# Attention and MoE on one Trainium2 core: the scaled words of the weights' decoding go to a PSUM bank

## The chip, the cores and the metric

The kernel runs on one core of a Trainium2 chip. The metric is the device time of one execution in microseconds (us). Engines: TensorE (PE, with its weight loads PEld), VectorE (DVE), ScalarE (ACT), GpSimd (POOL) and SyncE (SP), which issues most DMA transfers.

## The reference

```python
# attention: q, k, v are (8 batches, 8 heads, 576, 64) in fp32
scores = scale * np.matmul(q, k.transpose(0, 1, 3, 2))
...
mask = (rel >= 0) & (rel < window)          # window = 128
scores = np.where(mask, scores + bias[None], -1000000000.0)
scores = scores - np.max(scores, axis=-1, keepdims=True)
attn = np.exp(scores)
attn = attn / (np.sum(attn, axis=-1, keepdims=True) + 1e-09)
return np.matmul(attn, v).astype(np.float32)
...
# MoE: x is the attention's output, (4608 tokens, 512)
h = x @ w_in                                # (512, 2048)
g = h * (1.0 / (1.0 + np.exp(-1.702 * h)))
return (g @ w_out).astype(np.float32)       # (2048, 512)
```

`bias` is a slope of each head times minus the distance of the two positions. `w_in` and `w_out` come in 64-bit floats.

## The kernel before, in words

**The work.** The FFN runs over chunks of 256 tokens. One *step* is one chunk with one of the 16 blocks of 128 hidden columns: twelve up products into an h_ps bank (L552), ScalarE's tanh (L557), VectorE's g (L558), a split of g in a high and a low part (gh on ScalarE L561, gl on GpSimd L562), and six down products into the two accumulators acc0 and acc1 (L571). All products run in fp32 by such splits, three products for one. A `Job` is a chunk with a range of blocks; the list of jobs sets the order of the steps: chunk 0 with blocks 0–7 (steps 0–7), chunk 1 with all 16 (8–23), chunk 0 with blocks 8–15 (24–31), chunk 2 from step 32, chunk 3 from step 48, and so on.

**The attention** is cut into units of a pair of heads, which feed the chunks' x. In the first two batches a "whole" unit takes 256, 256 or 64 queries: units 0–3 have queries 0–255 of batch 0 ("early"), 4–7 queries 256–511, 8–11 queries 512–575, and 12–23 are the same of batch 1. A unit passes stages: loads of q, k and V (`load`, `load_whole_v`), score products into s_ps and sb_ps (L324), bias and minimum on VectorE (L351), exponentials on ScalarE (L374), reciprocal and scaling (L392 to L402, shared out over three engines), transposes into t_ps (L419) with copies out to pw (L427), the mix, which is the product of pw with V (L476), and the copy of its result to x (L485). `tick` moves four units by a stage each; the main loop calls it by a pace worked out from when the chunks are due. The mix of units 4 and later goes to the tile x_ps, tag x_ps, one buffer; the early ones use the tag h_ps. From batch 2 on, `mix` and `sum_up` (L499, L520) use x_ps too.

**The weights.** `fetch_weights` (L199) loads a block of w_in and one of w_out, 512 KB each, as 64-bit words through SP's queue, in program order with the loads of the attention (`move`, L155). `decode` (L203) makes fp32 parts out of them, a *half* (one block of one matrix) at a time; w4 below stands for the two halves of block 4. ScalarE scales the top words with Prelu, so that the sign is kept and the exponent lands in its place (L211, into the tile wc, tag o, three buffers); VectorE shifts the low words by 29 (L212) and joins the two by a shift of wc by 3 and an or, in place (L213, "shift-and-or" below); ScalarE casts the result to the high part (L216); GpSimd subtracts that to the low part (L217). There are 32 halves. The first three are decoded inside the attention's first ticks (`DECODE_TICKS`), the rest in the main loop, spread by `need`; the first eight keep their place in the program (`pin`).

**The order.** A scheduler sets the order of each engine's instructions from the program, the tiles' dependencies and its own model of time; an engine runs its order strictly from the front. SP's loads keep program order. PSUM has eight banks, all in use: acc0, acc1, s_ps, two of t_ps, one of x_ps, two of h_ps. V of the whole units has three buffers (L264), and so have q and k (tags rq, rk).

Of the kernel before, what the change touches and what calls it, by code (L numbers as in the profile page):

```python
# [8 lines left out]
F32 = mybir.dt.float32  # L9
F32R = mybir.dt.float32r  # L10
BF16 = mybir.dt.bfloat16
I32 = mybir.dt.int32
I64 = mybir.dt.int64
AF = mybir.ActivationFunctionType
ALU = mybir.AluOpType
# [5 lines left out]
P = 128  # L21
# [121 lines left out]
def tile_kernel(ctx: ExitStack, tc: tile.TileContext, q0, k0, v0, qT, kT, v, w_in, w_out, out):  # L143
    nc = tc.nc
# [5 lines left out]
    ffn = ctx.enter_context(tc.tile_pool(name="ffn", bufs=2))  # L150
    ps = ctx.enter_context(tc.tile_pool(name="ps", bufs=1, space=PSUM))
# [51 lines left out]
    def decode(st, name, pin=lambda ins: ins):  # L203

        words = st.bitcast(I32).rearrange("p (m two) -> p m two", two=2)
        top, low = words[..., 1], words[..., 0]
        c = ffn.tile([P, 512], I32, name="wc", tag="o", bufs=3)

        pin(nc.scalar.activation(c.bitcast(F32), top.bitcast(F32), AF.Prelu, scale=2.0 ** -112, alpha=2.0 ** 32))  # L211
        pin(nc.vector.tensor_scalar(low, low, 29, None, ALU.logical_shift_right))  # L212
        pin(nc.vector.scalar_tensor_tensor(c, c, 3, low, ALU.logical_shift_left, ALU.bitwise_or))  # L213
        w = c.bitcast(F32)
        res = const.tile([P, 2, 512], F32R, name=name, tag=name)
        pin(nc.scalar.copy(res[:, 0], w))  # L216
        pin(nc.gpsimd.tensor_tensor(res[:, 1], w, res[:, 0].bitcast(F32), ALU.subtract))  # L217
        return res
# [425 lines left out]
    def decode_next():  # L644
        nonlocal halves
        g, ws = halves // 2, (w1, w2)[halves % 2]

        pin = [tc.keep_in_program_order] if halves < PINNED else []
        ws[g] = decode(ws[g], f"w{1 + halves % 2}_{g}", *pin)
        halves += 1  # L650
# [123 lines left out]
```

## Time and profile before

| | |
|---|---|
| median of 3 runs | 1064.5 us (1063.76 to 1065.91) |
| the profiled execution | 1068.36 us |
| its span | 1066.3 us |
| granted TensorE clock, mean | 0.995 |
| HBM read, written | 67.63 MB, 9.44 MB |
| DMA, mean over the span | 74 GB/s |
| first tanh of step 0, 8, 16, 32, 48 | 32.4, 93.3, 126.4, 192.9, 253.2 us |
| decoding, first and last Prelu | 19.3, 125.8 us |

How to read the profile: L is a line of the kernel. A group's row names line, engine, operation, "output tile <- input tiles" without buffer numbers, shape, and the count behind an x; then its busy time in us, the mean in ns, and the idle time of the engine just ahead with what ended it. In rows grouped by tile the three numbers are the shortest, median and longest duration in ns. Rows of the timeline begin with the start and the duration in us; several instructions of one line in a row are drawn together. In the views of waits "A <- B: 3.7, 5, 1.8" is A's wait for B in us, how often, and the longest; indented rows by tile name what an engine sat idle for ahead of that tile's instructions.

### The profile page before, as it was taken

Reading aid. Unit: us, or ns where it says so; the run is one execution under the profiler, and the core shown is the slowest. Engines: PE = TensorE matmul, PEld = TensorE weight load, DVE = VectorE, ACT = ScalarE, POOL = GpSimd, SP = SyncE. Lnnn points to the kernel's source line nnn. Section 1 sums busy time; section 2 is a strip of 40 time slices with the busy share of each in tenths; the row PEclk is TensorE's granted clock in tenths of the full one; section 3 lists DMA queues with packets and bytes.
Section 4 is the critical chain, followed back from the end, with each engine's and each line's share of the span. In section 5 each row is a group of like instructions: output and inputs, shape, how many; then the busy total and the mean of one; then the engine's idle time right before and its main releaser. Section 6 shows DMA issues by size and latency. Waiting matters only on the chain.

```text
span 1066.3 us, 21362 instructions
## 1 busy us (share of the span) xinstructions
PE 1052.9 (99%) x7041; PEld 929.1 (87%) x7041; DVE 660.5 (62%) x2117; ACT 597.2 (56%) x1811; POOL 603.5 (57%) x863
## 2 busy tenths in 40 slices
PE   9899999999999999999999999999999999999998
PEld 5567787889989999999999999999999999998987
DVE  6797522568887777545767668767877687313121
ACT  6879853466666565535555556655665656322222
POOL 4579933567676666554656557656666665323232
PEclk9899999999999999999999999999999999999999
DMA  8872001223222132102121223212222221000000
GB/s 307 281 261 73 25 22 56 73 67 96 75 76 81 51 102 67 57 14 71 54 79 52 71 62 91 66 60 78 79 63 85 57 78 28 20 2 20 1 21 20
DMA packets 88109, 78.45 MB, mean 74 GB/s; under 512 B 36800, under 2 KB 79296, under 8 KB 88000
## 3 DMA queue, kind: packets, MB, share of 16 engines
q1 hardware_dynamic: 82240, 67.14, 21.4%
q10 hardware_dynamic: 5760, 9.96, 2.6%
q8 instruction: 55, 0.90, 0.3%
q14 instruction: 54, 0.44, 0.1%
HBM read 67.63 MB, written 9.44 MB: 72 GB/s over the span
## 4 chain that ended last, share of the span: by engine, by line
PE 94%; DVE 3%; ACT 1%; DMA 1%; issue 1%; POOL 0%; SPq 0%; DVEq 0%; POOLq 0%; ACTq 0%
PE h_ps L552 38%; PE acc L571 37%; PE s_ps L334 5%; PE x_ps L499 5%; PE t_ps L442 4%; PE x_ps L476 2%; PE t_ps L419 1%; PE sb_ps L324 1%; PE s_ps L324 1%; DVE wc L213 1%; DMA rw<-w_out 1%; ACT pb L374 1%; DVE rec L392 0%; PE acc L189 0%; DVE rw L212 0%
## 5 line engine op out<-in xcount | busy, mean ns | idle before, releaser
L562 POOL TENSOR_TENSOR gl<-g,gh 128x256 fp32r<-128x256 f32 x288 | 218.0, 757 | 292.2 <-ACT gh L561 224.9
L552 PE MATMUL h_ps<-xh,w 128*128 128x256 f32 x2304 | 370.2, 284 | 1.1 <-POOL w L217 0.6
L552 PEld LDWEIGHTS h_ps<-xh,w 128*128 128x128 f32 x2304 | 328.5, 189 | 34.5 <-issue 2.8
L571 PE MATMUL acc<-w,gh 128*128 128x512 f32 x1152 | 324.9, 400 | 0.0
L558 DVE SCALAR_TENSOR_TENSOR g<-g,h_ps 128x256 f32<-128x256 f32 x288 | 119.6, 415 | 207.9 <-ACT g L557 206.5
L557 ACT ACTIVATE g<-h_ps 128x256 f32<-128x256 f32 x288 | 110.4, 383 | 229.4 <-PE h_ps L552 207.3
L571 PEld LDWEIGHTS acc<-w,gh 128*128 128x128 f32 x1152 | 196.5, 189 | 27.9 <-ACT g L557 0.3
L552 PE MATMUL h_ps<-xl,w 128*128 128x256 f32 x1152 | 194.6, 280 | 0.0
L561 ACT CAST gh<-g 128x256 fp32r<-128x256 f32 x288 | 116.9, 406 | 129.5 <-DVE g L558 121.1
L571 PE MATMUL acc<-w,gl 128*128 128x512 f32 x576 | 188.0, 401 | 0.0
L552 PEld LDWEIGHTS h_ps<-xl,w 128*128 128x128 f32 x1152 | 164.2, 188 | 6.0
L312 POOL TENSOR_TENSOR K<-rk,K 128x384 fp32r<-128x384 f32 (+1 forms) x120 | 109.0, 909 | 65.2 <-ACT Q L292 15.9
L381 ACT ACTIVATE pb<-pb,mins 128x256 f32<-128x256 f32 (+2 forms) x216 | 104.9, 487 | 43.8 <-DVE mins L362 40.1
L571 PEld LDWEIGHTS acc<-w,gl 128*128 128x128 f32 x576 | 92.6, 188 | 9.5 <-issue 0.9
L311 POOL TENSOR_TENSOR Q<-rq,Q 64x256 fp32r<-64x256 f32 (+1 forms) x120 | 83.1, 692 | 22.2 <-DVE K L310 4.9
L406 DVE TENSOR_SCALAR pb<-pb,rec 128x256 f32<-128x256 f32 (+2 forms) x216 | 91.8, 461 | 3.2
L362 DVE CUSTOM_DVE_ANT_0 pb<-s_ps,bias 128x256 f32<-128x256 f32 (+3 forms) x240 | 85.7, 377 | 4.1 <-PE s_ps L334 2.8
L392 DVE TENSOR_SCALAR rec<-sums 128x2 f32<-128x2 f32 (+3 forms) x144 | 48.5, 336 | 58.4 <-ACT pb L381 53.6
L334 PE MATMUL s_ps<-K,Q 128*128 128x256 f32 (+1 forms) x432 | 79.8, 289 | 0.4 <-DVE mins L362 0.4
L310 DVE CAST K<-rk 128x384 fp32r<-128x384 f32 (+1 forms) x120 | 52.5, 438 | 41.2 <-PE s_ps L334 34.2
L461 DVE TENSOR_TENSOR pl<-t_ps,ph 128x512 fp32r<-128x512 f32 (+2 forms) x120 | 72.2, 604 | 9.3 <-ACT ph L455 6.6
L442 PE MATMUL t_ps<-ident,pb 128*128 128x128 f32 x408 | 74.2, 272 | 0.0
(68 smaller groups left out, 1322.2 us busy)
## 6 DMA issues: line engine op xcount, KB each, us to landing
rk<-kT SPq DMA_DIRECT2D x72, 192.0 KB, 2.5
rq<-qT SPq DMA_DIRECT2D x96, 128.0 KB, 2.3
out<-o ACTq DMA_DIRECT2D x36, 256.0 KB, 2.1
rw<-w_in SPq DMA_DIRECT2D x16, 512.0 KB, 6.5
rw<-w_out SPq DMA_DIRECT2D x16, 512.0 KB, 7.0
rk<-kT SPq DMA_DIRECT2D x48, 128.0 KB, 2.2
rv<-v SPq DMA_DIRECT2D x96, 64.0 KB, 1.9
rq<-q SPq DMA_DIRECT2D x16, 128.0 KB, 2.6
```

The source lines that it names most:

```text
L312: nc.gpsimd.tensor_tensor(K2, rk, K1.bitcast(F32), ALU.subtract)
L334: nc.tensor.matmul(u.s[:b.rows, e, b.first:b.end], u.Q[:, b.q0 - u.q0:b.q0 - u.q0 + b.rows], k[:, ko:ko + b.end - b.first], start=(z == 0) ...
L362: nc.vector.tensor_tensor_reduce(b.p[ra:rb, cs:b.end], u.s[ra:rb, e, cs:b.end], bias[head][ra:rb, cs:b.end], -SCALE, BIG, ALU.add, ALU.min ...
L381: nc.scalar.activation(live, live, AF.Exp, bias=u.mins[:b.rows, e:e + 1], scale=-1.0, accum_out=u.sums[:b.rows, e:e + 1],)
L406: nc.vector.tensor_scalar(live, live, u.rec[:rows, e:e + 1], None, ALU.mult)
L442: nc.tensor.transpose(u.t[:c.n, w:w + b.rows], b.p[:b.rows, col:col + c.n], ident[:b.rows, :b.rows])
L552: nc.tensor.matmul(h, w1[f][:, z, k * P:(k + 1) * P], x[:, k], start=(n == 0), stop=(n == len(ops) - 1))
L557: nc.scalar.activation(g, h, AF.Tanh, scale=0.851)
L558: nc.vector.scalar_tensor_tensor(g, g, 1.0, h, ALU.add, ALU.mult)
L561: nc.scalar.copy(gh, g)
L562: nc.gpsimd.tensor_tensor(gl, g, gh.bitcast(F32), ALU.subtract)
L571: nc.tensor.matmul(acc, g[:, t * P:(t + 1) * P], w2[f][:, z], start=(f == self.f0 and n == 0), stop=(f == self.f1 - 1 and n == 2))
```

## The change

`decode` gets a second tile. The scaled words go to c_ps, a PSUM tile of tag x_ps with its one buffer; the shift-and-or reads them there and writes the SBUF tile wc. The number of instructions is the same. Lines from L208 on are one higher in the changed kernel.

```diff
-        c = ffn.tile([P, 512], I32, name="wc", tag="o", bufs=3)
+        c = ps.tile([P, 512], I32, name="c_ps", tag="x_ps", bufs=1)
+        wc = ffn.tile([P, 512], I32, name="wc", tag="o", bufs=3)
...
         pin(nc.scalar.activation(c.bitcast(F32), top.bitcast(F32), AF.Prelu, scale=2.0 ** -112, alpha=2.0 ** 32))
         pin(nc.vector.tensor_scalar(low, low, 29, None, ALU.logical_shift_right))
-        pin(nc.vector.scalar_tensor_tensor(c, c, 3, low, ALU.logical_shift_left, ALU.bitwise_or))
-        w = c.bitcast(F32)
+        pin(nc.vector.scalar_tensor_tensor(wc, c, 3, low, ALU.logical_shift_left, ALU.bitwise_or))
+        w = wc.bitcast(F32)
```

With one buffer for the decoding and the mixes, the scheduler orders the engines anew. SP's order is the same in both. Counted up to the end of step 8's products, TensorE's order has 56 of the first two batches' 80 score products before and 41 now, 87 and 68 of 144 transposes, 60 and 40 of 112 mix products; by step 48 all are issued in both. The last Prelu stands at about step 17 before and step 22 now.

ScalarE before, around the second half of w2 and the halves of w3 (w1_3 is the high part of block 3 of w_in, w2_3 that of w_out, rw the loaded words, xf_697 the x that chunk 1 takes, pw a transposed unit):

```order
L216 CAST w2_2_580<-wc_576 128x512
L211 ACTIVATE wc_587<-rw1_3_258 128x512
L485 COPY xf_697<-x_ps_879 128x256
L427 COPY pw_846<-t_ps_845 128x512
L427 COPY pw_853<-t_ps_852 128x512
L399 ACTIVATE pb_865<-pb_865,rec_870 64x192
L557 ACTIVATE g_716<-h_ps_703 128x256
L216 CAST w1_3_591<-wc_587 128x512
L211 ACTIVATE wc_594<-rw2_3_260 128x512
L211 ACTIVATE wc_633<-rw1_4_318 128x512
```

ScalarE now, from the first half of w4 to the Prelu of w5 (x_ps_700 is unit 4's mix):

```order
L212 ACTIVATE c_ps_641<-rw1_4_318 128x512
L562 CAST gh_729<-g_726 128x256
L558 ACTIVATE g_826<-h_ps_813 128x256
L217 CAST w1_4_646<-wc_642 128x512
L212 ACTIVATE c_ps_649<-rw2_4_320 128x512
L562 CAST gh_829<-g_826 128x256
L217 CAST w2_4_654<-wc_650 128x512
L428 COPY pw_760<-t_ps_759 128x512
L486 COPY xf_707<-x_ps_700 128x256
L428 COPY pw_767<-t_ps_766 128x512
L212 ACTIVATE c_ps_743<-rw1_5_379 128x512
```

By then the order before had copied out the mixes of units 4, 5 and 6; now unit 4's copy is the first, behind w4, and a copy of a mix stands ahead of each following block's first Prelu.

TensorE before, at unit 4's mix (x_ps_690), which stands in step 0 (w1_0 is block 0):

```order
L552 MATMUL h_ps_538<-xl_529,w1_0_387 128x256 x4
L324 MATMUL sb_ps_496<-rk_249,rq_248 128x256
L324 MATMUL s_ps_495<-rk_249,rq_248 128x256
L324 MATMUL sb_ps_496<-rk_249,rq_248 128x256
L419 MATMUL t_ps_647<-ident_73,pb_475 128x128 x2
L476 MATMUL x_ps_690<-pw_459,VV_334 64x128
L476 MATMUL x_ps_690<-pw_466,VV_334 64x128
L476 MATMUL x_ps_690<-pw_459,VV_334 64x256
```

TensorE now, at the same mix (x_ps_700), between the products of steps 3 and 4:

```order
L572 MATMUL acc0_629<-w2_3_606,gh_829 128x512
L572 MATMUL acc1_630<-w2_3_606,gh_829 128x512
L572 MATMUL acc0_629<-w2_3_606,gh_829 128x512
L572 MATMUL acc1_630<-w2_3_606,gh_829 128x512
L477 MATMUL x_ps_700<-pw_461,VV_334 64x128
L477 MATMUL x_ps_700<-pw_468,VV_334 64x128
L477 MATMUL x_ps_700<-pw_461,VV_334 64x256
L477 MATMUL x_ps_700<-pw_468,VV_334 64x256
L477 MATMUL x_ps_700<-pw_461,VV_334 64x128
L477 MATMUL x_ps_700<-pw_468,VV_334 64x128
L553 MATMUL h_ps_905<-xh_531,w1_4_646 128x256 x4
```

The mix has moved behind four of step 3's down products and ahead of step 4's up products, which wait behind it.

## The prediction

> **What bounds the kernel now.** I read the page first: rows 1 and 2, the busy time of each engine over the span and in 40 slices of 26.7 us.
>
> ```profile
> PE 1052.9 (99%) x7041; PEld 929.1 (87%) x7041; DVE 660.5 (62%) x2117; ACT 597.2 (56%) x1811; POOL 603.5 (57%) x863
> PEld 5567787889989999999999999999999999998987
> ACT  6879853466666565535555556655665656322222
> DMA  8872001223222132102121223212222221000000
> ```
>
> TensorE bounds the kernel. Its matmuls overlap so far that the PE row can't show its idle time; the weight loads (PEld) can. They are busy at nine tenths in the later slices and at five to eight in the first nine, where the weights are decoded and ScalarE and the DMA engines are fullest. So the change must be priced there. The windows view gives stretches by step: steps 0–8, 8–16, 16–32, 32–48, and for comparison 600 us behind the decoding (columns: stretch, length, busy time of PE, PEld, DVE, ACT and POOL with instructions, granted clock, DMA share, GB/s).
>
> ```profile
> 32.40:93.20 60.80, 54.40 (x337) 38.43 (x338) 53.82 (x129) 50.80 (x158) 44.69 (x39) 0.92 0.67 229
> 93.20:126.30 33.10, 33.10 (x209) 25.27 (x208) 18.96 (x59) 32.55 (x95) 30.54 (x28) 1.00 0.18 50
> 126.30:192.80 66.50, 66.50 (x411) 51.86 (x410) 18.22 (x56) 31.39 (x99) 27.62 (x34) 1.00 0.13 37
> 192.80:253.10 60.30, 60.30 (x416) 53.67 (x416) 40.70 (x133) 35.88 (x116) 36.27 (x54) 1.00 0.25 72
> 300.00:900.00 600.00, 599.51 (x4112) 551.37 (x4111) 424.63 (x1411) 342.54 (x1050) 369.22 (x568) 1.00 0.24 67
> ```
>
> The bounds are tanh starts; the two ends of steps 0–8, from the timeline:
>
> ```profile
> 32.44 0.39 ACT L557 ACTIVATE g<-h_ps 128x256 f32<-128x256 f32 x1
> 93.32 0.43 ACT L557 ACTIVATE g<-h_ps 128x256 f32<-128x256 f32 x1
> ```
>
> My yardstick is the last stretch: 551.37/600 = 0.919 of PEld where PE rarely waits. PEld time over 0.919 is then a stretch's PE work, the rest its holes (slow-clock time counts as a hole). Steps 0–8: 38.43/0.919 = 41.8 of work, 19.0 of holes. Steps 8–16: 27.5 and 5.6. Steps 16–32: 56.4 and 10.1. Steps 32–48: 58.4 and 1.9. Some 37 us of holes in all are what any change here can gain, or add to.
>
> The decoding's own rows, grouped by tile, with what left an engine idle ahead of them:
>
> ```profile
> L211 ACT ACTIVATE wc<-rw x32: 654/682/722, 19.3 to 125.8; 128x512 f32<-128x512 f32 x32
> L213 DVE SCALAR_TENSOR_TENSOR wc<-wc,rw x32: 656/790/2514, 20.0 to 127.4; 128x512 int32<-128x512 int32 x32
> L216 ACT CAST w<-wc x32: 607/624/672, 20.7 to 129.1; 128x512 fp32r<-128x512 f32 x32
> L217 POOL TENSOR_TENSOR w<-wc,w x32: 1266/1288/2787, 21.4 to 131.4; 128x512 fp32r<-128x512 f32 x32
>   ACT wc L211: 9.4, 8
>   DVE wc L213: 4.6, 7
> ```
>
> VectorE's shift-and-or is stretched (median 790 ns, at most 2514) where ScalarE's instructions keep their time. ScalarE waits for it 4.6 us in all, at 7 of 32 halves.
>
> **The operation itself.** The shift-and-or gets one PSUM operand instead of two SBUF ones. The nearest rows are fp32 operations of VectorE of the same 128x512 shape that read PSUM:
>
> ```profile
> L584 DVE TENSOR_TENSOR o<-acc,xf x2: 681/686/692, 194.1 to 194.7; 128x512 f32<-128x512 f32 x2
> L587 DVE TENSOR_SCALAR o<-acc x34: 668/684/693, 161.7 to 1062.3; 128x512 f32<-128x512 f32 x34
> ```
>
> Neither is stretched in 36 instances, so I take 0.69 us; bounds are 0.656 (shortest today) and 0.79 (today's median). [...]
>
> ScalarE's write of c to PSUM has no row; its other 128x512 work lies between 0.58 and 0.75, and I leave it at 0.68. That is worth at most 0.1 us a half, either way.
>
> **The bank.** The new tile takes the only bank of tag x_ps, in which the 28 units of the first two batches mix, the first four apart. Where the decoding ran beside the mixes, with three SBUF buffers, every half now takes its turn: Prelu, shift-and-or, then the next half or a mix and its copy out. ScalarE and TensorE work in order, so two things queue behind a turn: behind a Prelu that waits for a mix, ScalarE's tanh, exponentials and copies; behind a mix that waits for a shift-and-or, the next up and down products. The scheduler has reacted. In the changed order 41 of 80 score products, 68 of 144 transposes and 40 of 112 mixes stand before the end of step 8, against 56, 87 and 60. TensorE's work for them:
>
> ```profile
> L476 PEld LDWEIGHTS x_ps<-pw,VV 128*64 128x64 f32 (+1 forms) x224 | 15.4, 143 | 12.5 <-issue 6.5 <-ACT g L557 1.4 <-ACT xh L536 0.6
> L419 PEld LDWEIGHTS t_ps<-ident,pb 128*128 128x128 f32 (+2 forms) x144 | 15.3, 138 | 11.3 <-issue 4.1 <-POOL pb L402 2.0 <-ACT w L216 1.2
> L324 PEld LDWEIGHTS sb_ps<-rk,rq 64*128 64x128 f32 (+1 forms) x80 | 11.4, 183 | 5.9 <-ACT pw L427 2.4 <-issue 1.1 <-ACT gh L561 0.4
> L324 PEld LDWEIGHTS s_ps<-rk,rq 64*128 64x128 f32 (+1 forms) x80 | 11.2, 181 | 6.7 <-DVE mins L351 2.7 <-issue 1.3 <-DVE rec L392 0.6
> ```
>
> 15/80 of 22.6, 19/144 of 15.3 and 20/112 of 15.4 make 4.2 + 2.0 + 2.7 = 9.0 us, 9.8 by the yardstick. This work filled holes that are there anyway, and comes back at steps 8–40, where there are fewer.
>
> **Steps 0–8, walked.** The ninth and the seventeenth Prelu (w4 and w8) start near 57.4 (the second of the first row's two) and at 80.9:
>
> ```profile
> 56.80 1.24 ACT L211 ACTIVATE wc<-rw 128x512 f32<-128x512 f32 x2
> 80.89 0.68 ACT L211 ACTIVATE wc<-rw 128x512 f32<-128x512 f32 x1
> ```
>
> Up to w4 the changed order has no mix in the bank, and the slow shift-and-or that ScalarE waits for 1.76 us there goes:
>
> ```profile
> 53.73 2.51 DVE L213 SCALAR_TENSOR_TENSOR wc<-wc,rw 128x512 int32<-128x512 int32 x1
> 56.27 0.62 ACT L216 CAST w<-wc 128x512 fp32r<-128x512 f32 x1 [1.76 <-DVE wc L213]
> ```
>
> The weights' arrival keeps part of that, so I take 1.0 off: 56.4. Then each of w4–w7 is a chain through the bank: Prelu 0.68, shift-and-or 0.69, the cast that stands ahead of the next Prelu 0.62, Prelu 0.68, shift-and-or 0.69, together 3.36; a wait of 0.6 to 1.0 until PE has run the four down products in front of the mix; the mix; then ScalarE's copies ahead of the next Prelu:
>
> ```profile
> 67.33 1.11 PE L571 MATMUL acc<-w,gh 128*128 128x512 f32 x4
> 60.74 1.77 PE L476 MATMUL x_ps<-pw,VV 128*64 128x128 f32 x12
> 65.35 0.60 PE L476 MATMUL x_ps<-pw,VV 128*64 128x64 f32 x8
> 36.87 0.35 ACT L485 COPY xf<-x_ps 128x256 f32<-128x256 f32 x1
> 37.12 0.58 ACT L427 COPY pw<-t_ps 128x512 f32<-128x512 f32 x1
> ```
>
> The 12 products lie partly in half-clock time, the 8 are of a smaller unit: 1.1 between them. The copies are 1.5 in w4 (two of pw beside that of x). That is 3.36 + 1.0 + 1.1 + 1.5 = 7.0 for w4; w5 with the wait at 0.6 takes 6.6; w6 and w7, with shorter copies, 5.9 and 5.7. In all 25.2 against 23.5 today, so w8's Prelu starts at 81.6. Then come the casts of chunk 1's x, its remainder and the up products:
>
> ```profile
> L536 ACT CAST xh<-xf x12: 387/400/448, 86.0 to 248.0; 128x256 fp32r<-128x256 f32 x12
> ```
>
> Four casts are 1.6; with a remainder on VectorE and the twelve products I take 4.9, an estimate (today it is 7.3 from the first cast at 86.0, with attention work between). Tanh 8 starts at 86.5, where it was 93.3.
>
> So steps 0–8 take 54.1 us, with 41.8 − 9.8 = 32.0 of work: holes of 22.1, **+3.1**.
>
> **Later steps.** In 8–16 ScalarE was full (32.55 of 33.10). The changed order has 58 ScalarE instructions there instead of 78, so PE holds the pace more often; holes between today's 5.6 and 1.0 (8 steps at the 1.9 of steps 32–48); 4.0, nearer the upper end since two halves a step still pass the bank: **−1.6**. In 16–32 the decoding runs to about step 22 instead of 17 and shares the bank with the mixes: holes from 10.1 to 11.1, **+1.0** (bounds −2 and +4). From step 48 on both orders have issued the same attention work, and 32–48 had few holes: 0, at most +2.
>
> Sum: +2.5 us. The profiled execution took 1068.36 us (span 1066.3) and becomes 1070.9; the median of the runs is 1064.5, 3.9 lower, and becomes 1067.0 with no change of scale.
>
> **The rivals.** A measurement here can tell about 0.2% (2.1 us) from no change.
>
> *Faster: the bank is free when wanted.* ScalarE's order has 91 instructions in steps 0–8 instead of 129, by their shapes 12.3 us less of its 50.8. If its idle time stays at today's 10.0 rather than growing by the turns, tanh 8 starts at 32.4 + 38.5 + 10.0 = 80.9. Holes: 48.5 − 32.0 = 16.5, −2.5, with the later terms −3.1: 1061.4, down to 1059 if 8–16 reaches 1.0. For it: a good part of that idle is the stretched shift-and-or (4.6). Against: the chain of 3.36 and a mix has no slack in it. It decides from a mean turn under 5 us.
>
> *Slower, by a loop through the loads.* The first mix (unit 4) moves from 37 us to about 60. The V load of unit 7 waits for its buffer, and on SP's queue w11's loads stand behind that V load; on VectorE w11's shifts stand ahead of w6's shift-and-or, which w6's mix waits for. The same holds one unit and one weight later.
>
> ```profile
> SPq L155 <- PE x_ps L476: 11.3, 6, 3.5
> rw<-w_in SPq DMA_DIRECT2D x16, 512.0 KB, 6.5
> rw<-w_out SPq DMA_DIRECT2D x16, 512.0 KB, 7.0
> ```
>
> Two steps of the chain are 11.4 to 13.6; the loop is the landing plus about 5.5 (two shifts, two shift-and-ors, a Prelu, the wait and a mix). So it decides where a pair of weights lands over 6–8 us after the mix: today's medians are at that point, though in a full queue. With a landing of 9 us each of two rounds costs 2 to 3 more: 1067.0 + 5 = 1072, to 1075.
>
> *The shift-and-or doesn't get shorter* (another reason for its stretch). Its group has a mean of 1017 ns:
>
> ```profile
> L213 DVE SCALAR_TENSOR_TENSOR wc<-wc,rw 128x512 int32<-128x512 int32 x32 | 32.4, 1017 | 9.5 <-ACT wc L211 9.4
> ```
>
> At that mean instead of 0.69, over the eight halves of w4–w7: +2.6, 1069.6.
>
> *Same:* the holes added early are taken back as steps 16–32 refill 10.1 us of holes with the deferred work, which PE could do in any order: 1064.5 to 1066.
>
> *The clock.* Half-clock time is already there:
>
> ```profile
> 38.30:45.10 6.80, 6.80 (x27) 4.29 (x24) 4.92 (x11) 5.12 (x15) 4.99 (x5) 0.50 0.61 185
> 58.80:62.20 3.40, 3.40 (x19) 2.80 (x20) 3.26 (x9) 3.06 (x9) 1.81 (x2) 0.50 0.99 352
> ```
>
> With work taken out of steps 0–8 another stretch of 3.4 us may fall in: +1.7. It widens the upper end only.
>
> **The numbers.** My forecast, 1067.0, has a chance of 0.30; the loop 0.10; the unshortened shift-and-or 0.05: slower 0.45. Same 0.27. Faster 0.28. The slow cases reach 1075 and with the clock 1077; the fast one 1059; with a tenth left out on either side the range is 1058.5 to 1076.
>
> **What would show it.** Right: the shift-and-or near 0.69 with hardly any spread; tanh 8 at about 86; ScalarE idle over 13 us in steps 0–8, ended by PE's mixes; PE waiting for the shift-and-or at L477; attention work in steps 16–40. Wrong: tanh 8 before 82 with ScalarE idle under 11; or shifts of w11 and w12 that wait for their DMA with VectorE idle, which is the loop; or a Prelu far off 0.68.

## The result, and the profile after

The changed kernel takes 1080.0 us (1078.9 to 1080.6, 4 runs) against 1064.2 (1063.8 to 1065.9, 4 runs): a ratio of 1.0144, 95% interval 1.0127 to 1.0162. It is slower, as forecast, but by 15.9 us where 2.5 were forecast, and outside the range. Its profiled execution has a span of 1078.5 us, 12.2 more than before; the difference to 15.9 is there because before's profiled execution, 1068.36 us, lies 4.2 above its median.

First the operation itself, grouped by the tile c_ps (shortest, median and longest ns; then VectorE's idle time until the Prelu, and that of ScalarE's casts until the shift-and-or):

```profile
L212 ACT ACTIVATE c_ps<-rw x32: 617/636/668, 19.2 to 139.1; 128x512 f32<-128x512 f32 x32
L214 DVE SCALAR_TENSOR_TENSOR wc<-c_ps,rw x32: 675/690/693, 19.9 to 139.9; 128x512 int32<-128x512 int32 x32
  ACT c_ps L212: 16.0, 14
  ACT w L217: 8.2, 12
```

The shift-and-or has lost its spread (675 to 693 ns, before 656 to 2514), and the Prelu is 46 ns shorter (median 636, before 682). Yet ScalarE waits for the shift-and-or 8.2 us at 12 halves, before 4.6 at 7: a half may no longer run ahead of another.

The windows view by tanh starts, steps 0–8, 8–32 and 32–48, first of before (PE, PEld, DVE, ACT, POOL busy, clock, DMA share, GB/s):

```profile
32.44:93.32 60.88, 54.48 (x338) 38.51 (x337) 53.94 (x129) 50.88 (x158) 44.77 (x39) 0.92 0.67 228
93.32:192.88 99.56, 99.56 (x618) 77.05 (x617) 37.06 (x114) 63.82 (x193) 58.04 (x61) 1.00 0.15 42
192.88:253.16 60.28, 60.28 (x417) 53.70 (x416) 40.76 (x133) 35.94 (x117) 36.28 (x55) 1.00 0.25 72
```

The same of after:

```profile
32.23:90.57 58.34, 47.51 (x248) 32.04 (x249) 35.64 (x92) 39.83 (x108) 34.51 (x33) 0.87 0.59 194
90.57:187.02 96.45, 96.45 (x610) 77.49 (x610) 38.59 (x128) 65.85 (x199) 52.25 (x59) 0.99 0.16 51
187.02:263.58 76.56, 76.56 (x511) 61.94 (x510) 40.14 (x142) 44.64 (x153) 40.65 (x60) 1.00 0.26 75
```

Up to step 32 the changed kernel is 5.9 us *ahead*. Steps 32–48 then take 16.3 us more, for 94 more TensorE instructions. They are the attention that was put off; in the windows of L477's mixes alone, after and before:

```profile
187.02:263.58 76.56, 8.87 (x74) 1.00 0.26 75
```

```profile
192.88:253.16 60.28, 2.18 (x24) 1.00 0.25 72
```

With 26 more transposes (4.1 us) and 16 score instructions where there were none (3.8) they are 14.6 us of PE busy time more. Where they come from, the same windows show. PE busy time of the attention's products (L476, L419 and L324 before, one line higher after) in us, beside the lengths of the stages:

| | steps 0–8 | 8–32 | 32–48 |
|---|---|---|---|
| attention's PE busy time, before | 30.21 | 32.97 | 3.14 |
| the same, after | 20.37 | 28.04 | 17.71 |
| its change | −9.84 | −4.93 | +14.57 |
| change of the stage's length | −2.54 | −3.11 | +16.28 |

So the work costs in steps 32–48 about what it cost in the earlier ones, and most of the loss arises where it was taken out: steps 0–8 gave back 2.5 of 9.8 us, steps 8–32 3.1 of 4.9. Steps 32–48 took 1.7 us more than their added work, and all that lies behind step 48 took 1.8 us longer. In steps 0–8 the granted clock is 0.87 instead of 0.92. One turn of the chain on ScalarE, w4's second Prelu to w5's first:

```profile
58.39 0.63 ACT L212 ACTIVATE c_ps<-rw 128x512 f32<-128x512 f32 x1
58.95 0.39 ACT L562 CAST gh<-g 128x256 fp32r<-128x256 f32 x1
59.84 0.63 ACT L217 CAST w<-wc 128x512 fp32r<-128x512 f32 x1 [0.50 <-DVE wc L214]
61.70 0.59 ACT L428 COPY pw<-t_ps 128x512 f32<-128x512 f32 x1 [1.23 <-PE x_ps L477]
62.19 0.38 ACT L486 COPY xf<-x_ps 128x256 f32<-128x256 f32 x1
62.45 0.60 ACT L428 COPY pw<-t_ps 128x512 f32<-128x512 f32 x1
62.92 0.66 ACT L212 ACTIVATE c_ps<-rw 128x512 f32<-128x512 f32 x1
63.48 0.40 ACT L558 ACTIVATE g<-h_ps 128x256 f32<-128x256 f32 x1
```

From the end of a shift-and-or at 59.8 to the Prelu at 62.92 no half is in the bank: it is the mix's, TensorE comes to the mix only behind four down products (59.58 to 60.59), and the mix's copy stands between two others. From w4's to w8's first Prelu it is 28.7 us (55.5 to 84.2). On VectorE, the shift-and-or of w5's first half then stands behind the minimum of a late score product:

```profile
63.78 0.35 DVE L352 CUSTOM_DVE_ANT_0 pb<-sb_ps,bias 64x192 f32<-64x192 f32 x1 [3.97 <-PE sb_ps L325]
64.06 0.68 DVE L214 SCALAR_TENSOR_TENSOR wc<-c_ps,rw 128x512 int32<-128x512 int32 x1
```

And the loop through the loads was there. SP's queue, with its last weight at 43.90 and the next transfer only behind unit 4's mix, then VectorE at w13's shifts ahead of w8's shift-and-or:

```profile
43.90 1.01 SPq L155 DMA_DIRECT2D rw<-w_out  x1
61.74 0.38 SPq L155 DMA_DIRECT2D VV<-v  x1
```

```profile
85.00 0.43 DVE L213 TENSOR_SCALAR rw<-rw 128x512 int32<-128x512 int32 x1 [2.34 <-DMA rw<-w_in]
86.85 0.43 DVE L213 TENSOR_SCALAR rw<-rw 128x512 int32<-128x512 int32 x1 [1.43 <-DMA rw<-w_out]
87.20 0.68 DVE L214 SCALAR_TENSOR_TENSOR wc<-c_ps,rw 128x512 int32<-128x512 int32 x1
```

w8's Prelu had ended at 84.87; its shift-and-or began 2.3 us later.

### The profile page after: what moved, and what is told of

The parts are those of the page before. It is cut to its first block, busy times and chain, and to the rows that moved or that the text cites. A ratio compares the mean times of both kernels' runs of the same rounds, so it can differ in the third digit from the quotient of the medians.

```text
span 1078.5 us, 21389 instructions
## 1 busy us (share of the span) xinstructions
PE 1059.0 (98%) x7041; PEld 931.5 (86%) x7041; DVE 647.6 (60%) x2117; ACT 597.7 (55%) x1811; POOL 592.0 (55%) x863
## 4 chain that ended last, share of the span: by engine, by line
PE 94%; DMA 2%; DVE 1%; ACT 1%; SPq 1%; issue 1%; DVEq 0%; POOL 0%; POOLq 0%; ACTq 0%
PE h_ps L553 38%; PE acc L572 37%; PE s_ps L335 5%; PE x_ps L500 5%; PE t_ps L443 4%; PE x_ps L477 2%; DMA rw<-w_out 2%; PE sb_ps L325 1%; PE t_ps L420 1%; PE s_ps L325 1%; SPq L155 1%; PE acc L189 0%; DMA rk<-k 0%; ACT pb L375 0%; DVE rw L213 0%
## 5 line engine op out<-in xcount | busy, mean ns | idle before, releaser
L553 PE MATMUL h_ps<-xh,w 128*128 128x256 f32 x2304 | 374.0, 285 | 6.2 <-ACT w L217 4.9
L563 POOL TENSOR_TENSOR gl<-g,gh 128x256 fp32r<-128x256 f32 x288 | 215.8, 750 | 272.2 <-ACT gh L562 217.9
L313 POOL TENSOR_TENSOR K<-rk,K 128x384 fp32r<-128x384 f32 (+1 forms) x120 | 108.8, 906 | 74.2 <-ACT Q L293 13.1
L572 PEld LDWEIGHTS acc<-w,gl 128*128 128x128 f32 x576 | 92.8, 188 | 9.2 <-issue 0.8
L393 DVE TENSOR_SCALAR rec<-sums 128x2 f32<-128x2 f32 (+3 forms) x144 | 44.3, 307 | 65.3 <-ACT pb L382 52.4
L443 PE MATMUL t_ps<-ident,pb 128*128 128x128 f32 x408 | 74.5, 272 | 0.0
L311 DVE CAST K<-rk 128x384 fp32r<-128x384 f32 (+1 forms) x120 | 49.3, 411 | 38.4 <-PE s_ps L335 31.6
```

Source lines behind the costliest of these rows:

```text
L313: nc.gpsimd.tensor_tensor(K2, rk, K1.bitcast(F32), ALU.subtract)
L443: nc.tensor.transpose(u.t[:c.n, w:w + b.rows], b.p[:b.rows, col:col + c.n], ident[:b.rows, :b.rows])
L553: nc.tensor.matmul(h, w1[f][:, z, k * P:(k + 1) * P], x[:, k], start=(n == 0), stop=(n == len(ops) - 1))
L563: nc.gpsimd.tensor_tensor(gl, g, gh.bitcast(F32), ALU.subtract)
L572: nc.tensor.matmul(acc, g[:, t * P:(t + 1) * P], w2[f][:, z], start=(f == self.f0 and n == 0), stop=(f == self.f1 - 1 and n == 2))
```

## The experiments

Four things came together: the operand, the turn in the shared bank, the loop and the clock. The table gives the medians, the ratio to before on the same chip with its interval (before's medians beside e1 to e15 were 1064.8 to 1065.7 us), three stages, w4's to w8's first Prelu, and the holes of steps 32–48 by the prediction's yardstick (length less PEld/0.919).

| run | median us | ratio | 0–8 | 8–32 | 32–48 | w4–w8 | holes 32–48 |
|---|---|---|---|---|---|---|---|
| before | 1064.2 | | 60.9 | 99.6 | 60.3 | 23.5 | 1.8 |
| after | 1080.0 | 1.0144 (1.0127–1.0162) | 58.3 | 96.5 | 76.6 | 28.7 | 9.2 |
| e1 | 1075.2 | 1.0091 (1.0061–1.0121) | 60.4 | 97.4 | 69.7 | 22.9 | 6.7 |
| e2 | 1063.6 | 0.9985 (0.9974–0.9997) | 46.7 | 94.5 | 74.2 | 19.5 | 7.7 |
| e3 | 1064.3 | 1.0000 (0.9985–1.0015) | 56.6 | 102.2 | 54.9 | 21.1 | 0.0 |
| e4 | 1075.7 | 1.0092 (1.0070–1.0114) | 53.2 | 95.5 | 76.6 | 29.1 | 9.1 |
| e5 | 1082.0 | 1.0162 (1.0138–1.0186) | 65.4 | 102.3 | 64.5 | 27.2 | 1.2 |
| e6 | 1074.6 | 1.0092 (1.0073–1.0112) | 56.5 | 103.5 | 60.5 | 23.0 | 0.4 |
| e7 | 1077.3 | 1.0121 (1.0098–1.0144) | 54.5 | 98.7 | 74.1 | 17.7 | 8.8 |
| e8 | 1073.9 | 1.0080 (1.0057–1.0103) | 58.2 | 99.7 | 69.7 | 17.8 | 6.7 |
| e9 | 1078.2 | 1.0116 (1.0090–1.0142) | 53.6 | 96.2 | 76.6 | 29.7 | 9.2 |
| e10 | 1068.3 | 1.0027 (1.0008–1.0047) | 54.4 | 91.5 | 69.2 | 23.5 | 7.0 |
| e11 | 1071.6 | 1.0063 (1.0041–1.0084) | 56.5 | 93.6 | 70.1 | 24.4 | 6.9 |
| e12 | 1073.5 | 1.0084 (1.0055–1.0113) | 61.3 | 92.8 | 70.4 | 21.5 | 7.8 |
| e13 | 1083.2 | 1.0173 (1.0153–1.0193) | 57.1 | 97.5 | 76.6 | 25.6 | 9.2 |
| e14 | 1065.1 | 1.0007 (0.9996–1.0017) | 56.6 | 103.3 | 54.6 | 24.1 | 0.2 |
| e15 | 1073.4 | 1.0093 (1.0073–1.0113) | 51.1 | 95.3 | 74.5 | 27.6 | 9.1 |

**The bank to itself (e1, e2).** Against before and after, both have

```diff
-            x = ps.tile([P, 4 * P], F32, name="x_ps", bufs=1)
+            x = ps.tile([P, T], F32, name="x_ps", tag="h_ps", bufs=2)
```

in `mix_whole`; e1 with the words in SBUF, e2 with them in PSUM.

> The kernel before, with the mixes of units 4 to 23 in the two h_ps banks instead of the x_ps bank; the scaled words stay in SBUF. Its order, too, puts attention off: 45 scores, 72 transposes and 44 mixes by step 8, against 56, 87, 60 before and 41, 68, 40 in the changed kernel. Theory A (attention put off is dear when it comes back, at steps 32 to 40, whatever put it off): about as slow as the changed kernel, 1074 to 1082, with steps 32 to 48 over 70 us. Theory B (the turns in the bank make the decoding slow in steps 0 to 8): no turns here, so 1064 to 1068.

> The changed kernel with the mixes of units 4 to 23 in the h_ps banks, so that the scaled words have their PSUM bank alone; order nearly that of the run before. Against that run it has only the operation's new operand. Theories A and B: 0 to 5 us faster than the run before, since the shift-and-or goes from a mean of 1.0 to 0.69. Rival C (the PSUM operand or the PSUM write itself costs the time): slower than the run before by 8 or more.

e1 lies in theory A's range, though its steps 32–48 (69.7) fall just short of the 70 named; theory B's range for it is out. e2 is 11.6 us faster than e1, more than either had, and 16.4 faster than the changed kernel. Rival C is out. Steps 0–8 of e2:

```profile
32.29:79.00 46.71, 41.62 (x270) 29.76 (x271) 37.91 (x105) 40.77 (x123) 36.37 (x33) 1.00 0.79 274
```

This is the "faster" rival's forecast (80.9) to 2 us: with no mix in the bank the decoding takes 19.5 us from w4 to w8. Nearly as much attention is put off as in the changed kernel (in the traces 88 of 224 instructions of mixes stand ahead of tanh 8, there 80, before 120), and still there is no loss: steps 32–48 are 14 us longer than before, but here the early steps give it back, 14.2 us in steps 0–8 and 5.1 in 8–32. In e1's profile the same steps took 60.4 us at a clock of 0.86, and its shift-and-or ran up to 3.5 us, so part of the 11.6 is the clock and not the operand: (1 − 0.86) x 60.4 = 8.5 us lost to the half clock, none in e2. One run of each had a granted clock of 0.994 over its whole span: e1's took 1071.5 us, e2's 1066.3. That leaves about 5 for the operand.

**Another bank (e3).** The words beside the up products' sums:

```diff
-        c = ps.tile([P, 512], I32, name="c_ps", tag="x_ps", bufs=1)
+        c = ps.tile([P, 512], I32, name="c_ps", tag="h_ps", bufs=2)
```

> The changed kernel with the scaled words in the two h_ps banks, beside the up products' sums, instead of the mixes' bank. Its order keeps the attention early (57, 90 and 60 by step 8), but the up products now share banks with the decoding. Theory A: steps 32 to 48 near 60 us again, the whole 1058 to 1068. Theory B (what costs is that a half takes turns in a bank with TensorE's work): the turns are now with the up products, which stand on the main path, so 1072 or more. Rival C: 1075 or more.

As theory A has it, with the attention early steps 32–48 fall to 54.9. But 8–32 rise to 102.2, and it ends level with before. Theory B's 1072 did not come: a turn with an up product is shorter than one with a mix. That is argued, not shown.

**The loop (e4, e8).** In the changed kernel and in e2:

```diff
-FETCH_AHEAD = 6
+FETCH_AHEAD = 16
```

> The changed kernel with all weights fetched ahead (FETCH_AHEAD 16 instead of 6), so that no weight stands behind a V load on the SP queue; TensorE's order is counted the same as in the changed kernel. Takes away the loop through the loads alone. Theory A: tanh 8 comes 2 to 3 us earlier (the shift-and-or of w8 waited 2.3 for w13's load in the profile), and the end 1 to 3 earlier: 1077 to 1079. Theory D (the loop through the loads makes most of the loss): 1068 or less.

> The run with the words alone in their bank and the mixes in the h_ps banks (1063.6), with all weights fetched ahead as well (FETCH_AHEAD 16). If the loop through the loads costs wherever mixes are late: 3 to 5 us faster, 1059 to 1061. If it only costs together with the turns: 1062 to 1066.

e4 gains 4.4 us, more than the 1 to 3 of theory A, and theory D falls. Tanh 8 stands at 85.7 instead of 90.6, with 29.1 us from w4 to w8 (28.7). Of this, 2.5 us come between w8's Prelu and tanh 8 (3.9 instead of 6.4 us), where the changed kernel waited for w13's load: that is the loop. Another 2.8 are there already at w4 (52.7 instead of 55.5), ahead of the first mix in the bank; there the changed kernel's profile has 10.2 us at half clock from 34.2 on, e4's none before 45.2. So the loop is real, but its own share is nearer 2.5 than the rival's 5, and the rest of the gain may be the clock. In e8 the same edit costs 10.3 us. Its mixes are as late as e2's (88 instructions ahead of tanh 8), but its profile has steps 0–8 at a clock of 0.82, e2's at 1.00: about 10 us of 58.2. The trace shows the longest pause ahead of tanh 8: at 76.28 up products have waited 5.34 us for ScalarE's copy of a mix out of the h_ps bank (75.86), which stands behind the casts and Prelus of the decoding, and a half-clock stretch sets in at 75.1, the second of 10.2 us there (the first at 34.1). So e8 doesn't tell what the loop costs in e2.

**The place in the program (e5, e6).** In the changed kernel and in the one before:

```diff
-SLACK = 2
+SLACK = 14
```

> The changed kernel with SLACK 14 instead of 2: the program calls the attention's ticks earlier, so that the mixes stand earlier among the decodings and get the bank sooner (one buffer is granted in program order). 49 scores, 78 transposes, 52 mixes by step 8 and all by step 40; with every turn in the bank as before. Theory E (the loss comes from the place in the program at which a mix gets the bank, which puts the attention off to steps 32 to 40): steps 32 to 48 below 66 us instead of 76.6, the whole 1066 to 1074. Theory B (the turns themselves are too long a chain): more turns fall into steps 0 to 16, which get longer by what steps 32 to 48 lose: 1077 to 1083.

> The control of the run before: the kernel before with SLACK 14; words in SBUF, 57 scores, 87 transposes and 60 mixes by step 8. Both theories: within 4 us of the kernel before, 1061 to 1068, since its order was early anyway.

Theory E got the stage right (64.5, holes 1.2) and the whole wrong; theory B's 1077 to 1083 came true. Pulled forward, the mixes lengthen steps 0–8 from 58.3 to 65.4. The control missed its range, too: the edit itself costs 10 us, some 4 of them behind step 96 (641 us instead of 637). Against that control the bank costs 7.4.

**Parts of the change (e7, e12).** In e7 the first nine halves go through the bank; e12 has `halves >= 18` there:

```diff
-        c = ps.tile([P, 512], I32, name="c_ps", tag="x_ps", bufs=1)
         wc = ffn.tile([P, 512], I32, name="wc", tag="o", bufs=3)
+        c = ps.tile([P, 512], I32, name="c_ps", tag="x_ps", bufs=1) if halves < 9 else wc
```

> Only the first nine halves (w0 to the first half of w4) write their scaled words to the mixes' bank, the other 23 to SBUF as before. Takes the turns from w4's second half on away, and keeps the first mix behind w4 as in the changed kernel. Theory B (turns of w4 to w8 and the loop make the loss): 1064 to 1069. Theory E (the late first mix makes the loss): at least half of it stays, 1071 to 1078.

> Only the halves from w9 on write their scaled words to the mixes' bank, the first 18 to SBUF as before. The mixes of units 4 to 7 stand ahead of them in the program and need no turn, those from unit 8 on do. Theory E (late first mixes make the loss): below 1070. Theory G (any turn in the bank puts attention off to steps 32 to 40; here 45, 72, 44 by step 8): 1071 to 1079, with steps 32 to 48 over 68 us.

Either part gives most of the loss: 12.4 and 7.8 us, and both have steps 32–48 over 70. Theory B falls for e7, and theory E for e12, where G was right. The table's last column sorts all runs: where the mixes share a bank, with the halves, the up products or the transposes, steps 32–48 hold 6.7 to 9.2 us of holes by the yardstick; where they have it alone (before, e3, e6, e14), and in e5, where the program calls them earlier, under 2. Where the halves share it, the reason can be read off the trace: the one buffer is granted in the program's order, and there unit 4's mix stands behind the tenth half, unit 5's behind the twelfth, and unit 8's behind the nineteenth (their copies follow the Preludes of these halves). Before, the mixes' bank was theirs alone, and the scheduler ran them far ahead of that. Why sharing with up products or transposes has the same effect in steps 32–48 was not tested apart.

**The clock (e9).** In `up`, ahead of the twelve products, for the first eight steps:

```diff
+            if now < 8:
+                m = ident.bitcast(BF16)
+                for _ in range(6):
+                    nc.tensor.matmul(h, m[:, :P], m, start=True, stop=True)
```

> The changed kernel with six idle products (bf16, of the identity, into the h_ps bank that the up products then overwrite) ahead of the up products of steps 0 to 7, where TensorE waits for the weight's cast; attention by step 8 as in the changed kernel (41, 68, 40). In its profile TensorE lost 8.5 us to the half clock in steps 0 to 12, against 4.9 before. Theory F (the half clock makes a good part of the difference): the loss falls under 2 us and the whole to 1071 to 1076. Against: the clock only slows what waits anyway, 1078 to 1083.

Steps 0–8 are back at 0.97 and 4.7 us shorter, though their first tanh is 2.4 later:

```profile
34.59:88.23 53.64, 44.87 (x289) 32.66 (x290) 31.62 (x86) 39.00 (x106) 32.22 (x31) 0.97 0.60 199
```

The whole gains 1.8 us only (3.3 against before on the same chip), hardly more than the runs scatter, so theory F falls: the half clock of steps 0–8 is a small part of the loss, 1.8, or 4.2 if the late start is the idle products' own price.

**The operand, once more (e10, e11).** e1 and e2 with the mixes in the t_ps banks.

> The changed kernel with the mixes of units 4 to 23 in the two banks of the transposes (t_ps), so that the scaled words have their bank alone and the attention stays early (57, 84, 60 by step 8). If turns in the bank are what costs: 1056 to 1066, and faster than its control. If the PSUM operand only gains where it keeps the clock up: as its control, within 3 us.

> The control of the run before: the kernel before with the mixes of units 4 to 23 in the t_ps banks; words in SBUF; 53, 78 and 53 by step 8. 1062 to 1072: mixes and transposes now share two banks.

By the medians the operand gains 3.3 us here. The profiled executions, both at a clock of 1.00 in steps 0–8, differ by 7.1 (1064.4 and 1071.5): e10's ten runs go from 1064.4 us at a granted clock of 0.999 to 1073.8 at 0.989. The two orders differ as well, so the size stays between 3 and 7. e10 missed its range by 2 us, and its attention was early by step 8 only: steps 32–48 still have 50 instructions of mixes, before 24. With the operand in PSUM the shift-and-or's longest is 692 to 699 ns (the changed kernel, e2 to e5, e7, e8, e10).

**The turn without the operand (e13, e14).** The kernel before, in which 8 of 512 columns go another way; e14 has `k = c`:

```diff
+        k = ps.tile([P, 512], I32, name="c_ps", tag="x_ps", bufs=1)
...
-        pin(nc.scalar.activation(c.bitcast(F32), top.bitcast(F32), AF.Prelu, scale=2.0 ** -112, alpha=2.0 ** 32))
+        pin(nc.scalar.activation(k[:, :8].bitcast(F32), top[:, :8].bitcast(F32), AF.Prelu, scale=2.0 ** -112, alpha=2.0 ** 32))
+        pin(nc.scalar.activation(c[:, 8:].bitcast(F32), top[:, 8:].bitcast(F32), AF.Prelu, scale=2.0 ** -112, alpha=2.0 ** 32))
```

and the shift-and-or is cut likewise.

> The turn without the operand: the kernel before, in which the first 8 of a half's 512 columns go through the mixes' PSUM bank (a small Prelu ahead, a small shift-and-or behind the large one) and the other 504 stay in SBUF. A half holds the bank as long as in the changed kernel; 41, 68 and 40 by step 8, the changed kernel's counts. Theory B (turns): 10 or more above its control. Theory H (the operand in PSUM is the cost): within 3 us of its control.

> The control of the run before: the same two small instructions a half, all columns in SBUF, no bank; 57, 87 and 60 by step 8. 64 small instructions more on ScalarE and VectorE: 1063 to 1072.

This tells turn and operand apart. The turn alone, with the order that it brings, turns 1065.1 into 1083.2, 18.1 us more, and the stages of e13 are the changed kernel's to within 1.3 us; theory H falls. Steps 32–48 of e13 and of e14:

```profile
187.84:264.44 76.60, 76.60 (x511) 61.98 (x510) 40.18 (x142) 44.81 (x154) 40.69 (x60) 1.00 0.26 75
```

```profile
193.16:247.72 54.56, 54.56 (x380) 49.95 (x379) 37.67 (x118) 31.39 (x98) 31.41 (x48) 1.00 0.23 66
```

The changed kernel, with the turn and the operand, is 3.2 us faster than e13 (2.4 if each is compared with before on its own chip).

**Turn and operand alone (e15).** The edits of e4 and e9 together.

> The changed kernel with all weights fetched ahead and the six idle products a step: neither the loop through the loads nor most of the half clock is left, only the turns (41, 68, 40 by step 8). If the parts add up: 1080.0 less 4.4 for the loop and 1.8 for the clock is 1073.8; 1071 to 1076. From w4's to w8's first Prelu still 28 us or more. If loop and clock are the whole cause: 1068 or less.

The parts add up: 1073.4 against 1073.8 worked out. With 27.6 us from w4 to w8, just under the 28 named, the turn is still there, and 8.4 us of loss against before on its chip.

So an account of the 15.9 us: fetching ahead 4.4 (the loop, with the clock mixed in), the idle products 1.8 (5.2 and 3.3 if each run is compared with before on its own chip), and the rest, 8.4 to 9.7, the turn with the order that it brings, the operand's gain already taken off. The root is shown, by e13 against e14: a bank that decoding and mixes share. How the rest divides between the longer chain and the attention put off is open: e7 has a short chain (17.7) and loses 12.4, and e1, in which no half shares a bank with a mix, loses 10.2. The loop runs through the late mix and so has the same root. For the clock that is not shown: e14, without the bank, has 1.00 in steps 0–8 where e13 has 0.85, but before has 0.92 and e1 0.86 without such a turn.

## Why the prediction was right or wrong

- *The operation*: right. 0.69 us, the PSUM rows' value, without spread (675 to 693 ns). From the shortest with two SBUF operands, 0.656, to the median with one in PSUM, 0.690, it is 34 ns more. What stretched the one with two SBUF operands, to 2.51 us before and 3.68 in e11, no run tells. The operand was worth some 3 to 5 us by the pairs above, and that was not where the time went. The rival of an unshortened shift-and-or is out.
- *The walk* is one of two steps that failed: steps 0–8 took 58.3 us where 54.1 were forecast. w4 came at 55.5 (56.4 forecast), but w4 to w8 took 28.7 (25.2): each block took 7.4, 7.4, 8.0 and 5.9 where 7.0, 6.6, 5.9 and 5.7 were forecast. Missing were the bias-and-minimum of a late score product, which stands ahead of the shift-and-or on VectorE (w5's began 0.5 us after its Prelu), and the half clock at w6's mix (1.98 us for 12 products, 1.09 at w5's). Tanh 8 came at 90.6 (86.5): most of the rest is w13's load. TensorE waiting for the shift-and-or at L477, named as a sign, did not show: it came to the bank late, and ScalarE waited for it. ScalarE's idle time in steps 0–8, 58.34 − 39.83 = 18.5, did (over 13 forecast); its waits for mixes make 5.3 of it, those for the shift-and-or 5.7. That the holes of steps 0–8 come so near, 23.5 (22.1), is luck: the weight loads fell by 6.5 us where 9.0 were forecast.
- *Steps 8–32*: holes 2.0 and 10.2 (4.0 and 11.1), both better than forecast.
- *Steps 32–48*: this is the other step that failed: "32–48 had few holes: 0, at most +2". They have 9.2 instead of 1.8, +7.4. The work put off was booked as coming back "at steps 8–40". None came back in steps 8–32: 4.9 us more of PE busy time left them, and all 14.6 landed in steps 32–48, where TensorE had been busy throughout, and which took 16.3 us longer. The order has only 72 of 80 score products, 112 of 144 transposes and 75 of 112 mixes by step 32. The yardstick made this look free: it measures weight loads, and 74 mixes have 5.15 us of loads to 8.87 of PE busy. So most of the +7.4 is work that the yardstick priced too low, not idle time. And behind step 48, where 0 was forecast, it is 1.8 us more.
- *The rivals as alternatives*: the loop was priced at +5; its sign showed (shifts waited 5.7 us for loads of w_in in steps 0–8), and fetching ahead gained 4.4, of which some 2.5 are the loop's. The clock was priced at +1.7 and measured 1.8 to 3.3. They were given chances of their own beside the forecast, but they were no alternatives: both held at once, and they add up. Forecast, loop and clock together would have been 1073.7, with the holes of steps 32–48 1081; this sum was made afterwards, and parts of it that missed cancel.
- *The "same" rival*: its refilling of steps 16–32 did not come; they have 10.2 us of holes, 10.1 before.
- *The "faster" rival*: its premise, a bank that is free when wanted, was wrong for this kernel and right for e2.

## What to carry to other kernels

A tile put into a bank that other work uses buys its faster operand, here a median of 690 instead of 790 ns, with a place in a queue, and with one buffer that queue has the program's order; look up what the program has ahead of each user before pricing the operation. Work that is put off costs its engine time again where it lands, here 14.6 us; whether the stage that it leaves gets shorter by as much depends on what else bounds that stage, here 2.5 of 9.8 us. Price both by PE time of those instructions, not by a share of loads. Rivals that can hold at once belong in one sum.

## What the runs showed of the hardware

- ScalarE's Prelu of 128x512 took 636 ns into PSUM and 682 into SBUF (medians of 32).
- The shift-and-or of 128x512 with two SBUF operands took 0.65 to 3.68 us (before, e1, e7, e11), with one in PSUM 0.65 to 0.70 (the changed kernel, e2 to e5, e7, e8, e10).
- Moderate edits that leave the work as it is change what steps 0–8 lose to the half clock between 0 (e2, e6, e10, e11, e14) and about 10 us (e8). Runs of one kernel differ as well: e10 took 1064.4 us at a granted clock of 0.999 and 1073.8 at 0.989.
- In steps 32–48 of the changed kernel 74 instructions of mixes had 5.15 us of weight loads to 8.87 us of PE busy time, where the kernel before, from 300 to 900 us, had 0.919 us of loads to one of time.

e2 is the one version here below before, by 0.15% (0.03 to 0.26%): hardly more than a measurement can tell.
